# A new hand-written instruction order for the first of two spectral + MLP layers, with the negated third of a table made earlier

## The chip, the cores and the metric

The kernel runs on one core of a Trainium2 chip. The core has a matrix engine (TensorE, PE in the profile), a vector engine (VectorE, DVE), an activation engine (ScalarE, ACT), a general engine (GpSimd, POOL) and a queue engine for transfers (SyncE, SP). The metric is the device time of one execution in microseconds; lower is better.

## The reference, cut to what matters

Two blocks, A and B, are applied twice in turn to a state `x` of 2048 rows and 512 columns (bf16).

```python
def _A_ref(x, w_r, w_i):                       # spectral filter
    X = rfft2(x.astype(float32))               # over rows and columns
    X = X * (w_r + 1j * w_i)                   # 2048 x 257 weights
    return irfft2(X, s=(S, D)).astype(bfloat16)

def _B_ref(x, w1, w2, w3, w4):                 # mixer and MLP, F = 1792
    h = gelu(layernorm(x) @ w1)
    # four column groups of h are shifted by +1, -1, +2, -2 rows
    x1 = x + concat(shifted h) @ w2
    return x1 + gelu(layernorm(x1) @ w3) @ w4

x = x + _A_ref(layernorm(x), w_r, w_i);  x = x + _B_ref(layernorm(x), w1, w2, w3, w4)
x = x + _A_ref(layernorm(x), w_r, w_i);  x = x + _B_ref(layernorm(x), w1, w2, w3, w4)
```

## The kernel before, in words

The 2048 rows are held as 128 partitions by 16 columns-of-rows, called q. The Fourier transforms are matrix products with tables. One call of `layer` is one spectral block and one MLP block; it is called twice, with the order string `ORDER_A` for the first layer and `ORDER_B` for the second. Nothing schedules the kernel but these strings (the tile framework is in manual schedule mode): a token is one step, steps are recorded in the order of the string, and each engine carries out its own steps in that order. The number after a dot is the PSUM bank (of eight) that a step's products write. A trailing A or V says whether ACT or DVE does a copy or a normalization.

The tokens, by stage:

- **Forward spectrum, weights, first half of the way back.** `d` (line 462, PE) transforms the columns of unit u (a unit is one or two of 16 frequency blocks b); `t` (ACT or DVE) copies the result out as `TV`; `q` (line 486, PE) does the rest of the row transform with the table `TL`; `x` copies it out as `X`; `p` (`weigh`, line 501, DVE) multiplies `X` by the weights `W`, once with the real plane (pl 0) and once with the imaginary one (pl 1), into `PB`; `b` (`back_q`, line 510, PE) multiplies `PB` by the table `TR`, eight products to a block; `m` (`take_b`) copies block b into `M`.
- **The made third of the table.** `TR` has three parts. Two are loaded from DRAM (line 180, in two halves of 16 frequencies), and the third is minus the first: `N0` and `N1` (`negate`, line 698, DVE) make it for blocks 0 to 7 and 8 to 15. Every second product of a `b` reads it.
- **Second half of the way back, first norm.** `D` (line 528, PE) needs all of `M`; `Y` copies out; `P` (line 540, PE); `a` (line 548, DVE) adds to x; `s` (line 258, ACT) sums squares; `r` and `c` (POOL) make the norm's factors for four q; `n` normalizes; `T` (SP) turns two q by a transposing DMA.
- **MLP.** `v` (line 579) is the product with w1, `h` its gelu (ACT), `u` (line 595) the product with w2 over shifted rows, `f`, `k`, `E`, `R`, `o`, `U` the residual and the second norm, `w` (line 630) the product with w3, `g` (line 637, ACT) its gelu, `W` (line 643) the product with w4, `A` (line 648, DVE) the add to x. `L` (`permute`, DVE) rearranges a part of `W` for the second layer.
- **Seam to the second layer.** `B`, `j`, `S` (statistics on DVE, factors on POOL), `Q` (DVE, a scaled table), `O` (lines 349 to 361, PE, the next layer's first transform), `G` (copies into `V`), `X` (zero products that fill PE). The second layer's first `d` needs all of `V`.

The small buffers are few, and a step that reuses one waits for its last reader: `TV` and `Y` share three, `X` has two, `PB` has eight slots (two to a `p`).

How the weights arrive: `load_all` queues all loads on SP in one fixed order, each chunk of `W` covering four blocks (blocks 0 to 3, 4 to 7, 8 to 11, 12 to 15), real plane first. A chunk lands in partitions 0 to 63, and a second DMA, issued by POOL (line 209), copies it to partitions 64 to 127. `weigh` needs both. After the last of them a small gate DMA (line 187) lets the four MLP weights start. Neither the loads nor the POOL copies are in the order string.

Of the kernel before, what the change touches and what calls it, by code (L numbers as in the profile page):

```python
# [13 lines left out]
BF16 = dt.bfloat16  # L14
FP32 = dt.float32

P = 128
# [81 lines left out]
def kernel(  # L99
# [26 lines left out]
    load_all(K, A_x, A_w_r, A_w_i, B_w1, B_w2, B_w3, B_w4)  # L126
    make_hT(K)
    wake(K)
    first_front(K)
    for last in (False, True):  # L130
# [88 lines left out]
def wake(K):  # L219

    nc = K.nc
    t = K.const.tile([P, 256], BF16, name="zeros")
    nc.vector.memset(t[:], 0.0)
    one = K.small.tile([P, 1], FP32, name="wake")
    nc.scalar.activation(one[:], K.eps[:], ACT.Sqrt, bias=0.0, scale=1.0)
    K.zeros = t
    fill(K, WAKE)


def fill(K, n):  # L230
    for i in range(n):
        K.nc.tensor.matmul(K.ps[:, 7 if K.bank is None else K.bank, 0:256], lhsT=K.zeros[:, 0:P], rhs=K.zeros[:], start=True, stop=True)


class Stats:
# [155 lines left out]
def first_front(K):  # L391
# [26 lines left out]
    def front(k):  # L418
        ps[k] = over_p(K, FIRST[k])
        if k in FILL:  # L420
            fill(K, FILL[k])
# [19 lines left out]
def layer(K, last):  # L441
# [265 lines left out]
    for op in (ORDER_B if last else ORDER_A).split():  # L707
        op, _, bank = op.partition(".")
        K.bank = int(bank) if bank else None
        if op[0] == "X":  # L710
            fill(K, int(op[1:]))
            continue
        if op[0] in FLEX:
            table[op[0]](int(op[1:-1]), op[-1])
        else:
            table[op[0]](int(op[1:]))
# [16 lines left out]
Q15V O3 Q14V G4A O5 G3V O7 G5A O8 G8A G7V  # L733
"""
ORDER_A = """
d4.0 d1.2 d2.4 t1A q1.2 t2A t4V x1V q4.0 d10.6 q2.4 x4A p1 t10V d6.2 d12.0 q10.6 x2A t6A p4 N0 d8.4 q6.2 t12A t8A
b1.0 x10V d15.1 p2 b4.6 b3.7 m1A x6A b5.0 m4A t15V d14.1 q8.2 m3A b2.6 p10 d0.7 m5A N1 p6 q12.4 b10.0 t14V x8A
q15.2 x12A t0A p8 m2A x15A b11.1 m11A p12 q0.4 b6.7 b8.6 m6A p15 x0A q14.2 x14V b7.1 m10A b9.7 m7A m9A b13.4 p0
b15.5 b12.0 p14 m15A m15V m12A b0.1 b14.7 m8V m13V m0A m14A D2.4 D3.6 Y3A D0.0 Y2V P4.4 a4 Y0A P7.5 P6.6 P5.7 D1.0
a7 a6 a5 D4.4 s4 P0.6 Y1V s7 P1.7 s6 a0 s5 P3.0 Y4A r1 a1 P2.1 s0 a3 P8.6 P9.7 a2 D5.4 a8 D7.0 n7V n6V n5V T3 s1  # L740
n4V s3 s2 T2 r0 a9 D6.2 Y5A P11.6 Y7A s8 P10.4 P15.5 Y6A P13.7 a11 a10 s11 n2V n3V a15 n0V P14.6 n1A a13 c1 s10
P12.4 s9 r2 a12 s15 L7 a14 v3.2 n10V s12 n9V s13 s14 T1 v2.4 h3 n8A T0 n11V L12 r3 h2 n12V v1.6 h1 v0.2 T5 h0 c0
n15V n14A u3.6 T4 u2.7 u1.2 v5.4 f1 n13V u0.3 L15 h5 v4.0 f2 T7 T6 f3 E2 f0 u4.2 E3 v6.6 h4 k1 f4 L6 L1 v7.2 k3
u5.0 E4 c3 u6.1 k0 f5 E0 u7.4 k2 c2 R0 h7 h6 E1 o0V f6 k4 o1V o2A u10.5 u9.0 f7 u8.1 o3V u14.4 u12.6 f10 k5 f8
u11.1 U0 L9 k6 k7 f9 u13.5 R1 E5 u15.0 f12 E7 f14 f13 U1 E9 E8 w4.6 o4A E6 f11 L5 o5V o6V o7A w0.4 k10 k8 k9 w5.2
g0 E13 w1.4 f15 E14 k12 U3 E11 k11 k13 U2 g4 E12 k14 w2.0 E10 w6.6 R2 g5 w7.2 g1 o9V g7 o11V g6 k15 w3.4 g2 o10A R3
g3 o8A L0 w13.2 w9.6 w12.0 L3 w11.4 o14A E15 U4 g13 g12 L10 o13V U5 g11 W1.0 g9 W2.1 W3.6 L11 o15A w10.4 w8.2 L4
g10 o12V L2 L13 A1 g8 L8 A3 A2 W0.4 w14.2 A0 B2 W5.5 B0 L14 B3 g14 U6 W7.4 A5 B1 A7 B7 w20.2 w19.4 j1 j2 W6.0 j0 j7
g19 W4.1 U7 A6 g20 w15.2 w24.4 w21.6 B5 A4 g21 g15 w16.0 B6 j3 B4 w17.6 w23.2 g16 j6 w27.0 j5 g17 g27 w18.6 j4 g18
S0 w25.0 Q0 W9.6 Q3 S1 W10.7 g25 A10 g24 Q2 B10 w22.4 W8.7 Q1 g23 A9 Q4 O1.2 g22 Q7 w26.4 Q6 B9 W11.6 O0.0 G1A j9  # L750
Q5 g26 G1V A8 B8 O2.4 G0A A11 B11 G2A j11 W14.7 W12.6 j10 G2V A14 B14 j14 j8 G0V A12 S14 Q14 B12 W15.7 j12 A15 B15
j15 W13.6 O14.7 S2 S12 Q9 Q11 O3.0 Q12 S15 Q8 Q10 O4.4 G14A G3A Q15 A13 B13 G4A j13 G3V S13 O5.6 X4.2 O15.2 Q13 G4V
G15V G5A G15A X4.3 O6.6 G6A X8.3
"""
ORDER_B = """
d15.0 t15A d4.2 q15.0 x15V d1.4 t4A d8.6 t1A q1.4 q4.2 p15 t8A x1V b15.0 d12.6 x4A p1 m15V m15A q8.4 t12A d10.0
# [45 lines left out]
```

## Time and profile before

| | us |
|---|---|
| median of 13 runs | 368.7 |
| lowest and highest of them | 366.07 and 369.82 |
| the profiled execution | 368.84 |
| its span in the profile | 366.9 |
| PE busy in the span | 344.6 (94%) |
| DVE busy | 183.7 (50%) |
| ACT busy | 198.9 (54%) |
| POOL busy | 67.0 (18%) |
| granted TensorE clock, mean | 0.986 |

All times in this text are microseconds from the start of the span of that one execution. Busy is the time in which an engine has an instruction in work[...]. In a timeline row, the first number is the start, the second the length, `x8` the number of instructions merged, and the bracket how long the engine had been idle and who ended that.

The first layer's frequency stage runs from 22.91 (first `d`) to 52.99 (first `D`), its middle up to 98.24 (first `w`), its MLP up to about 196.4 (last `W`), and the second layer's first `d` starts at 202.71.

### The profile page before, as it was taken

The page shows a single profiled execution, that of the slowest core. Times are in us where ns is not written, and L with a number is a line of the kernel's source. Part 1 is how long each engine was busy: PE and PEld are TensorE (multiplying, and loading weights), DVE is VectorE, ACT ScalarE, POOL GpSimd, SP SyncE. Part 2 cuts the span into 40 slices and gives each one's busy share as a digit, 9 for nine tenths or more (in the row PEclk, how much of TensorE's full clock was granted, in tenths as well). Part 3 has the DMA queues.
Part 4 walks back from the last instruction along what each step waited for, and adds up shares of the span by engine and source line. Part 5 has one row for each costly group of instructions (what it writes and reads, how often), then busy time and mean ns, then how long its engine had stood idle before and what let it go on. Part 6 is the DMA issues. An engine that isn't in the chain of part 4 may idle for free.

```text
span 366.9 us, 5596 instructions
## 1 busy us (share of the span) xinstructions
PE 344.6 (94%) x2107; PEld 189.8 (52%) x2124; DVE 183.7 (50%) x453; ACT 198.9 (54%) x343; POOL 67.0 (18%) x171
## 2 busy tenths in 40 slices
PE   7798599889999999999999999999999999999996
PEld 5576378534444444444446678734444444444442
DVE  4856568838985243400688697855690021100022
ACT  5867469978679230154213897996786420247100
POOL 1211003782341000200022000782440000000000
PEclk9899889999999999999999999999999999999999
DMA  7999493641332500000000000363313032000012
GB/s 232 232 202 214 105 372 123 114 87 30 58 58 38 107 0 2 0 0 2 1 0 2 2 2 0 61 115 59 57 30 58 0 57 73 0 29 2 29 43 86
DMA packets 47274, 24.60 MB, mean 67 GB/s; under 512 B 34832, under 2 KB 44048, under 8 KB 47248
## 3 DMA queue, kind: packets, MB, share of 16 engines
q1 hardware_dynamic: 46464, 22.09, 26.5%
q0 software_dynamic: 640, 2.10, 2.7%
q8 instruction: 16, 0.26, 0.3%
q14 instruction: 10, 0.08, 0.1%
q10 hardware_dynamic: 144, 0.07, 0.1%
HBM read 11.67 MB, written 2.10 MB: 38 GB/s over the span
## 4 chain that ended last, share of the span: by engine, by line
PE 73%; DMA 11%; ACT 9%; DVE 3%; issue 2%; SPq 1%; POOL 0%; ACTq 0%; DVEq 0%; POOLq 0%
PE ps L630 26%; PE ps L643 25%; PE ps L595 8%; PE ps L579 5%; ACT junk L258 4%; DMA W<-in_A_w_i_dram 3%; PE ps L510 3%; DMA W<-W 2%; DMA TL<-tab_TL 2%; PE ps L462 2%; DMA W<-in_A_w_r_dram 2%; PE ps L486 2%; PE ps L528 2%; ACT Y L149 1%; SPq L166 1%
## 5 line engine op out<-in xcount | busy, mean ns | idle before, releaser
L637 ACT ACTIVATE gT<-ps 128x1024 bf16<-128x1024 f32 x56 | 54.9, 1023 | 86.5 <-PE ps L630 86.5
L630 PE MATMUL ps<-xT,w 128*128 128x512 bf16 x448 | 98.7, 379 | 0.0
L643 PE MATMUL ps<-w,gT 128*128 128x512 bf16 x435 | 97.8, 379 | 0.7
L648 DVE TENSOR_TENSOR x_state<-ps,x_state 128x512 bf16<-128x512 f32 x32 | 21.7, 689 | 121.1 <-PE ps L643 121.0
L630 PEld LDWEIGHTS <-w 128*128 128x128 bf16 x448 | 43.8, 98 | 52.6
L643 PEld LDWEIGHTS <-gT 128*128 128x128 bf16 x448 | 43.8, 98 | 52.6
L579 PE MATMUL ps<-xT,w 128*128 128x512 bf16 x128 | 29.1, 379 | 1.5 <-ACT hT L586 0.9
L603 DVE SCALAR_TENSOR_TENSOR xn<-xn,ln_c,ps 128x512 bf16<-128x512 bf16 x32 | 23.1, 743 | 13.3 <-PE ps L595 9.0
L595 PE MATMUL ps<-w,hT 128*128 128x512 bf16 x124 | 28.8, 379 | 1.0 <-ACT hT L586 0.8
L501 DVE TENSOR_TENSOR PB<-X,W 128x1024 bf16<-128x1024 bf16 (+1 forms) x40 | 21.3, 579 | 7.8 <-DMA W<-W 4.2
L510 PE MATMUL ps<-TR,PB 128*128 128x128 bf16 x256 | 19.1, 232 | 5.6 <-DVE TR L698 4.6
L258 ACT ACTIVATE junk<-x_state 128x512 bf16<-128x512 bf16 x36 | 22.6, 629 | 1.1
L548 DVE SCALAR_TENSOR_TENSOR x_state<-ps,x_state 128x512 bf16<-128x512 f32 x32 | 20.4, 686 | 3.5 <-PE ps L540 3.5
L258 ACT ACTIVATE junk<-xn 128x512 bf16<-128x512 bf16 x32 | 20.1, 627 | 3.6 <-DVE xn L603 3.1
L586 ACT ACTIVATE hT<-ps 128x512 bf16<-128x512 f32 x32 | 17.5, 607 | 7.9 <-PE ps L579 7.9
L246 DVE BATCH_NORM_STATS2 ln_st<-x_state 128x6 f32<-128x512 bf16 x28 | 18.8, 685 | 4.8 <-DMA x_state<-in_A_x_dram 4.6
L510 PEld LDWEIGHTS <-PB 128*128 128x128 bf16 x256 | 16.3, 104 | 9.3 <-issue 4.8
L579 PEld LDWEIGHTS <-w 128*128 128x128 bf16 x128 | 12.4, 98 | 16.7 <-issue 1.5
L595 PEld LDWEIGHTS <-hT 128*128 128x128 bf16 x128 | 12.4, 98 | 16.4 <-ACT hT L586 1.1
L149 ACT ACTIVATE V<-ps 128x1024 bf16<-128x1024 f32 (+2 forms) x11 | 9.5, 885 | 15.8 <-PE ps L351 14.2
L281 POOL TENSOR_SCALAR ln_ve<-ln_mv 128x4 f32<-128x4 f32 (+1 forms) x15 | 3.9, 261 | 76.9 <-DVE ln_mv L274 76.2
L462 PE MATMUL ps<-FA,V 128*128 128x256 bf16 x128 | 16.3, 273 | 1.7 <-ACT V L149 1.7
(73 smaller groups left out, 389.0 us busy)
## 6 DMA issues: line engine op xcount, KB each, us to landing
w<-in_B_w_dram SPq DMA_DIRECT2D x2, 1792.0 KB, 12.3
x_state<-in_A_x_dram SPq DMA_DIRECT2D x8, 256.0 KB, 5.8
W<-W POOLq DMA_DIRECT2D x8, 256.0 KB, 8.8
out_dram<-x_state SPq DMA_DIRECT2D x16, 128.0 KB, 1.8
TR<-tab_TR SPq DMA_DIRECT2D x2, 512.0 KB, 10.0
w<-in_B_w_dram SPq DMA_DIRECT2D x2, 512.0 KB, 4.5
W<-in_A_w_r_dram SPq DMA_DIRECT2D x7, 128.0 KB, 11.0
W<-in_A_w_i_dram SPq DMA_DIRECT2D x7, 128.0 KB, 10.5
```

The source lines that it names most:

```text
L258: K.nc.scalar.activation(junk[:], src, ACT.Square, bias=0.0, scale=D ** -0.5, accum_out=self.s[:, i, 1:2])
L462: nc.tensor.matmul(oi[:, 1 - h], rhs=K.FA[:, t, h], lhsT=V[:, 2 * t + h, 2 * b:2 * b + 2].rearrange("d b q c -> d (b q c)"), start=(t == 0 ...
L501: nc.vector.tensor_tensor(t[:, :, 0:n], x, w, op=ALU.mult)
L510: nc.tensor.matmul(o[:, (2 * h + F) * P:(2 * h + F + 1) * P], lhsT=pab[u][k][:, h, b - u, F * P:(F + 1) * P], rhs=K.TR[:, k:k + 2, 2 * b + ...
L548: nc.vector.scalar_tensor_tensor(K.x[:, q, :], ps.pop(("P", q)), 1.0, K.x[:, q, :], op0=ALU.mult, op1=ALU.add, accum_out=ln[g].s[:, i, 0:1])
L579: nc.tensor.matmul(o[:, i], lhsT=K.w1[:, t, j * P:(j + 1) * P], rhs=xT[g][:, :, t, :], start=(t == 0), stop=(t == 3))
L595: nc.tensor.matmul(o, lhsT=K.hT[:, j, st:st + P], rhs=K.w2[:, j, :], start=(j == 0), stop=(j == 3))
L603: nc.vector.scalar_tensor_tensor(xn[:, q, :], xn[:, q, :], ln[q // 4].c[:, q % 4:q % 4 + 1], ps.pop(("u", n)), op0=ALU.mult, op1=ALU.add, ...
L630: nc.tensor.matmul(o[:, i], lhsT=K.w3[:, c, t * P:(t + 1) * P], rhs=xT3[g][:, :, c, :], start=(c == 0), stop=(c == 3))
L637: nc.scalar.activation(gT[g][:, 2 * j:2 * j + 2, :], ps.pop(("w", k)), ACT.Gelu_apprx_tanh, bias=0.0, scale=1.0)
L643: nc.tensor.matmul(o, lhsT=gT[g][:, t, i * P:(i + 1) * P], rhs=K.w4[:, t, :], start=(t == 0), stop=(t == 13))
L648: nc.vector.tensor_tensor(K.x[:, q, :], ps.pop(("W", n)), K.x[:, q, :], op=ALU.add)
```

## The change

`ORDER_A` is replaced by another order of the same steps, with other banks and here and there another engine for a copy. `ORDER_0` (everything before the first layer) and `ORDER_B` are untouched. In the frequency stage the first units are now 1, 0, 4, 6, 2; `N0` stands before `p4` instead of after it, and `N1` before `p10` instead of after it. The `p` steps come as 0, 1, 4, 6, 2, 10, 8, 12, 14, 15 (before: 1, 4, 2, 10, 6, 8, 12, 15, 0, 14). At the seam, row q = 0 (`W14`) is now the last product of the MLP instead of row 15 (`W13`), so `O14`, one row, comes last instead of `O6`, two rows. Apart from that the zero tile of the filling products is 128 columns instead of 256, read twice.

```diff
 def wake(K):
-    t = K.const.tile([P, 256], BF16, name="zeros")
+    t = K.const.tile([P, P], BF16, name="zeros")
 def fill(K, n):
     for i in range(n):
-        K.nc.tensor.matmul(K.ps[:, 7 if K.bank is None else K.bank, 0:256], lhsT=K.zeros[:, 0:P], rhs=K.zeros[:], start=True, stop=True)
+        K.nc.tensor.matmul(K.ps[:, 7 if K.bank is None else K.bank, 0:256], lhsT=K.zeros[:], rhs=K.zeros[:].unsqueeze(1).to_broadcast([P, 2, P]), start=True, stop=True)
 ORDER_A = """
-d4.0 d1.2 d2.4 t1A q1.2 t2A t4V x1V q4.0 d10.6 q2.4 x4A p1 t10V d6.2 d12.0 q10.6 x2A t6A p4 N0 d8.4 q6.2 t12A t8A
-b1.0 x10V d15.1 p2 b4.6 b3.7 m1A x6A b5.0 m4A t15V d14.1 q8.2 m3A b2.6 p10 d0.7 m5A N1 p6 q12.4 b10.0 t14V x8A
-q15.2 x12A t0A p8 m2A x15A b11.1 m11A p12 q0.4 b6.7 b8.6 m6A p15 x0A q14.2 x14V b7.1 m10A b9.7 m7A m9A b13.4 p0
-b15.5 b12.0 p14 m15A m15V m12A b0.1 b14.7 m8V m13V m0A m14A D2.4 D3.6 Y3A D0.0 Y2V P4.4 a4 Y0A P7.5 P6.6 P5.7 D1.0
-a7 a6 a5 D4.4 s4 P0.6 Y1V s7 P1.7 s6 a0 s5 P3.0 Y4A r1 a1 P2.1 s0 a3 P8.6 P9.7 a2 D5.4 a8 D7.0 n7V n6V n5V T3 s1
-n4V s3 s2 T2 r0 a9 D6.2 Y5A P11.6 Y7A s8 P10.4 P15.5 Y6A P13.7 a11 a10 s11 n2V n3V a15 n0V P14.6 n1A a13 c1 s10
-P12.4 s9 r2 a12 s15 L7 a14 v3.2 n10V s12 n9V s13 s14 T1 v2.4 h3 n8A T0 n11V L12 r3 h2 n12V v1.6 h1 v0.2 T5 h0 c0
-n15V n14A u3.6 T4 u2.7 u1.2 v5.4 f1 n13V u0.3 L15 h5 v4.0 f2 T7 T6 f3 E2 f0 u4.2 E3 v6.6 h4 k1 f4 L6 L1 v7.2 k3
-u5.0 E4 c3 u6.1 k0 f5 E0 u7.4 k2 c2 R0 h7 h6 E1 o0V f6 k4 o1V o2A u10.5 u9.0 f7 u8.1 o3V u14.4 u12.6 f10 k5 f8
-u11.1 U0 L9 k6 k7 f9 u13.5 R1 E5 u15.0 f12 E7 f14 f13 U1 E9 E8 w4.6 o4A E6 f11 L5 o5V o6V o7A w0.4 k10 k8 k9 w5.2
-g0 E13 w1.4 f15 E14 k12 U3 E11 k11 k13 U2 g4 E12 k14 w2.0 E10 w6.6 R2 g5 w7.2 g1 o9V g7 o11V g6 k15 w3.4 g2 o10A R3
-g3 o8A L0 w13.2 w9.6 w12.0 L3 w11.4 o14A E15 U4 g13 g12 L10 o13V U5 g11 W1.0 g9 W2.1 W3.6 L11 o15A w10.4 w8.2 L4
-g10 o12V L2 L13 A1 g8 L8 A3 A2 W0.4 w14.2 A0 B2 W5.5 B0 L14 B3 g14 U6 W7.4 A5 B1 A7 B7 w20.2 w19.4 j1 j2 W6.0 j0 j7
-g19 W4.1 U7 A6 g20 w15.2 w24.4 w21.6 B5 A4 g21 g15 w16.0 B6 j3 B4 w17.6 w23.2 g16 j6 w27.0 j5 g17 g27 w18.6 j4 g18
-S0 w25.0 Q0 W9.6 Q3 S1 W10.7 g25 A10 g24 Q2 B10 w22.4 W8.7 Q1 g23 A9 Q4 O1.2 g22 Q7 w26.4 Q6 B9 W11.6 O0.0 G1A j9
-Q5 g26 G1V A8 B8 O2.4 G0A A11 B11 G2A j11 W14.7 W12.6 j10 G2V A14 B14 j14 j8 G0V A12 S14 Q14 B12 W15.7 j12 A15 B15
-j15 W13.6 O14.7 S2 S12 Q9 Q11 O3.0 Q12 S15 Q8 Q10 O4.4 G14A G3A Q15 A13 B13 G4A j13 G3V S13 O5.6 X4.2 O15.2 Q13 G4V
-G15V G5A G15A X4.3 O6.6 G6A X8.3
+d1.0 d0.1 d4.2 t1A t0V q0.0 x0V q1.4 d6.6 x1V t4A p0 d2.0 t6A q4.4 d10.2 t2V q6.6 x4A p1 N0 p4 d8.4 t10A t8V x6A p6
+q2.0 b1.2 b4.3 m1A d12.6 b0.2 m4A d14.3 x2A q10.4 t12A p2 d15.0 b5.1 t14V x10A m0V q8.6 b2.3 b6.4 x8A m2A m6A m5A
+q12.6 q14.2 N1 p10 b7.5 t15A p8 b10.4 m7V b11.1 b3.0 x12A m11A x14V p12 p14 m3A b8.5 m8A q15.6 m10A b9.2 x15A p15
+b12.3 b13.5 m12A m9A b14.4 m13V b15.3 m15V m14A m15A D0.2 D1.4 Y1A Y0V D3.6 P1.2 P0.3 P2.4 a1 P3.5 Y3A a0 a2 a3
+D2.6 D4.2 Y2V P6.4 s1 P7.5 a6 a7 s0 P4.6 s2 P5.7 D7.0 s3 a5 a4 D5.4 r0 Y4A n2V s6 P8.7 s7 s5 P9.6 n3V s4 D6.2 Y7A
+n1V a8 Y5A n0V Y6A P10.7 r1 P11.4 a9 P13.5 a10 P15.6 T1 n5V T0 n4V n6A P12.7 n7V s10 a11 T2 T3 a12 s9 a15 P14.2 s11
+s8 a13 s13 s15 v0.0 c1 v1.4 a14 v3.2 s14 s12 r2 r3 c0 h1 n10V h0 v2.4 n11V h3 n9V T5 h2 n8V u0.2 n13V L3 n12A u1.3
+u2.4 n14A n15A T4 f0 v5.0 h5 T6 v4.6 E0 u3.2 f1 L5 f2 c2 u4.3 h4 L7 f3 k1 T7 E3 k2 u5.6 f4 k0 k3 R0 f5 v7.4 v6.6
+L13 E2 h7 u15.4 u7.5 k4 E1 f15 h6 o3V E4 u6.6 o0V E15 o1V k15 f6 u12.4 u11.7 f7 c3 f11 U0 o2A u8.6 k6 f8 u13.5 E5
+f13 k5 E11 u9.7 E8 k7 k8 u10.6 u14.5 k11 R1 U1 f9 E6 f12 f10 w6.2 o6A f14 E12 E7 E9 k10 L2 o5V w0.6 w3.4 L8 k9 E10
+o7V g0 R2 w5.6 k12 w4.0 E13 o4A k13 U2 g3 g4 w1.4 o9A E14 g1 o11V L15 w2.0 L6 L1 g5 k14 g2 R3 U3 w7.4 g6 w9.6 g7 L9
+w8.2 w10.4 g9 L12 o15A o8V W0.6 o12A g8 W3.7 o10V w12.2 A0 w13.0 L11 o13A W1.6 g13 g12 g10 A3 U4 o14V A1 w11.2 g11
+U5 w14.6 B3 W5.2 W7.3 W2.4 B0 A5 W4.2 L4 B5 A7 j3 j0 L14 B7 B1 W6.3 U7 A2 w15.4 A4 j1 g14 w17.6 g15 B2 A6 j5 j2
+w16.4 g16 U6 B6 B4 S0 Q1 w20.2 w18.4 g18 L0 g17 j7 w19.0 g20 w21.4 j4 j6 S1 Q7 Q2 g19 Q3 w24.2 Q4 w22.0 g21 O1.4
+G1A W9.6 g24 w26.2 g22 Q0 Q5 Q6 A9 G1V B9 w25.6 j9 w23.4 g26 g25 W10.6 W11.7 A10 g23 O3.4 G3A A11 B11 O2.2 L10 j11
+w27.0 B10 G3V W8.6 A8 B8 g27 j8 j10 W15.7 A15 W13.6 S2 O0.4 Q9 W12.7 G2A Q10 B15 G2V Q11 A13 G0A Q8 G0V W14.6 j15
+B13 O4.4 j13 A12 O5.2 S15 B12 Q15 S13 j12 O15.7 S12 Q13 Q12 G4A A14 B14 j14 G15V S14 Q14 G5A X4.0 O6.0 X4.6 O14.6
+G6A G4V G15A G14A X8.2
```

## The prediction

> **What bounds the kernel now.** I read the engine table first (PE 344.6 of 366.9), then the chain of waits that ended last, then the timelines of PE and DVE where PE was not full. PE is full from 80 to 196 and in the second layer's MLP. The order of the first layer can matter in three places: the frequency stage (22.91 to 52.99), the middle (to 98.24), and the seam (last `W` to 202.71).
>
> The chain through the frequency stage, in order of time (start, length, what):
>
> ```profile
> 19.43 12.36 DMA W<-in_A_w_i_dram
> ...
> 32.34 8.84 DMA W<-W
> ...
> 41.20 0.69 DVE PB L501
> 41.89 0.35 DVE TR L698
> ...
> 42.28 0.82 PE ps L510 x7
> ```
>
> The imaginary weights of blocks 8 to 11 are complete at 41.20. Behind them wait one multiplication (`p10`, second half), then `N1`, and only then PE. DVE and PE, from their timelines:
>
> ```profile
> 30.08 0.69 DVE L501 TENSOR_TENSOR PB<-X,W 128x1024 bf16<-128x1024 bf16 x1 [1.15 <-ACT TV L149]
> 31.58 0.69 DVE L501 TENSOR_TENSOR PB<-X,W 128x1024 bf16<-128x1024 bf16 x1 [0.81 <-DMA W<-W]
> ...
> 37.56 0.69 DVE L501 TENSOR_TENSOR PB<-X,W 128x1024 bf16<-128x1024 bf16 x1 [1.96 <-issue]
> 41.20 0.69 DVE L501 TENSOR_TENSOR PB<-X,W 128x1024 bf16<-128x1024 bf16 x1 [2.95 <-DMA W<-W]
> ```
> ```profile
> 32.66 0.55 PE L510 MATMUL ps<-TR,PB 128*128 128x128 bf16 x7 [1.00 <-DVE TR L698]
> ...
> 38.46 0.23 PE L510 MATMUL ps<-TR,PB 128*128 128x128 bf16 x1
> 42.28 0.82 PE L510 MATMUL ps<-TR,PB 128*128 128x128 bf16 x7 [3.60 <-DVE TR L698]
> ...
> 52.99 2.78 PE L528 MATMUL ps<-G,M 128*128 128x256 bf16 x24 [0.88 <-DVE M L147]
> ```
>
> All four DVE rows are `p4` and `p10` waiting for weights. The releasers of the first and third do not fit: the POOL copies of those planes were issued at 21.14 and 28.63, and 8.9 later (the imaginary one took 8.84) is 30.04 and 37.53. While DVE stood at `p10`, `p6` stood behind it, whose weights had been there since 31.58. PE was idle for 3.60, and paid again:
>
> ```profile
> 40.00:42.00 2.00, 0.00 (x0) 0.06 (x1) 0.80 (x2) 0.01 (x1) 0.00 (x0) 1.00 0.54 115
> 42.00:44.00 2.00, 1.39 (x11) 0.86 (x12) 2.00 (x5) 1.17 (x2) 0.00 (x0) 0.60 0.01 2
> 44.00:46.00 2.00, 1.46 (x12) 0.97 (x11) 2.00 (x5) 2.00 (x4) 0.00 (x0) 0.50 0.46 127
> 46.00:48.00 2.00, 2.00 (x20) 1.71 (x20) 1.20 (x3) 1.76 (x4) 0.00 (x0) 0.50 1.05 343
> 48.00:50.00 2.00, 2.00 (x26) 1.59 (x27) 1.43 (x4) 1.28 (x4) 0.00 (x0) 0.69 1.03 383
> ```
>
> (Busy of PE, PE weight load, DVE, ACT, POOL; then the granted clock.) It is about half from 42.5 to 49.2. Sixteen `b` products took 1.89 there and about 1.05 at full clock.
>
> **The change part by part.** Loads and POOL copies keep their order, so weights land as before: 30.05 and 31.58 (blocks 4 to 7), 37.5 and 41.20 (8 to 11), by about 42.9 (12 to 15: the gate behind them issued at 42.97). I walked the new order on all engines, each step at the latest of its engine, its input and its buffer's last reader, with row durations: a two-block `d` 0.95, `q` 0.54, `b` 0.53; ACT `t` 1.3, `x` 0.93, `m` 0.5; DVE `t` 1.3, `x` 1.2, `m` 0.65, two-block `p` half 0.62, `N` 0.35.
>
> *Blocks 0 to 7.* `p0` ends at 27.65 (its imaginary plane lands at 27.28, as in the old rows), `t2V` 28.9, `p1` 29.5, `N0` 29.85. `N0` now lies in the wait of `p4` for 30.05 and costs nothing; without that cover it is 0.35. `p4` still ends at 32.2, where `b4` waits 0.85 instead of 1.0 for `N0`. Then `t8V` 33.45, `p6` 34.7, `p2` 35.95, `t14V` 36.6, `m0V` 37.25, `N1` 37.6. `N1` needs the second half of `TR`: issued at 20.62, at most 13.1 to landing, so 33.7. It costs nothing ahead of `p10`, which waits for 37.53. On PE this feeds b1, b4, b0, b5, b2, b6, b7 and d12, d14, d15, q10, q8, q12, q14, up to 39.5. Then `b10` stands: 39.6 to 41.9, a gap of 2.3 instead of 3.6. Queued behind DVE's wait are `p8`, `m7V`, `x14V`, `p12`; all need later weights or are short.
>
> *After 41.20.* Old: PE had eleven `b` and three `q` left, DVE thirteen multiplications (six of half size), a `t`, an `x`, `N1`. New: nine `b` and one `q`; nine multiplications (four of half size): `p10` to 41.85, `p8` 43.1, `m7V` 43.7, `x14V` 44.35, `p12` 45.6, `p14` 46.25, `p15` 46.9. PE follows: b8 44.3, q15 44.6, b9 45.15, b12 46.2, b13 46.7, b14 47.25, b15 47.8. Last `m` 48.4. First `D` at **48.5** instead of 52.99: 4.5 less, some 3 of it the half clock.
>
> [...] The trace shows gaps up to 1.0 with the clock at 1.00 after, and 3.60 with half after; 2.3 lies between. [...] nine `b` costing 1.05 each: about 2.5 more, 51.0. In this trace 32 to 34 had PE busy 1.19 of 2.0 and the clock stayed 1.00, so I take 48.5 and keep 51.0.
>
> [...] `N1` and `p6` move to where POOL issues the copies at 32.34 and 36.42[...]. The row: the POOL copies took 509 to 775 ns, 512 in the middle, the one at 32.34 beside `N0` 0.51. I take nothing.
>
> *Middle, D to the first w: 45.25 before.* It is bound by ACT: six `Y`, sixteen `s`, one `n`, then the gelu table (1.28) at 72.80, 19.8 after the first `D`, without a gap from 54.94. The new order has the same six, sixteen and one there, and its first `Y` is also ready after two `D`, at 1.95. Then three `h` (1.0 each) open the first `u`: 24.1 (before: 24.4, with a normalization of 0.7 among the three). From there 16 `u` and 4 `v` at 0.216 a product are 20.7. **45.0**, -0.25. The transposes T1, T0 come at 59.0 by this clock; the MLP weights, gated at 43 as before, finish by 58.2 (DMA share 1.05 at 57, 0.27 at 58), so they just miss each other; overlap would cost at most v0's slack, about 0.6, before it counts. `N`, `L` and residuals moved on DVE lie in its idle time (50% busy).
>
> *MLP, 98.2 before.* 448 products at 0.216 are 96.7, and four `O` of 8 short products (0.45) stand before the last `W` instead of three: 98.5, +0.3 to +0.45. `g` takes 1.0 for each 1.73 of `w`; I found no `w` or `W` whose bank or gelu comes late.
>
> *Seam, 6.27 before (196.44 to 202.71).*
>
> ```profile
> 202.71 1.48 PE L462 MATMUL ps<-FA,V 128*128 128x256 bf16 x12 [1.01 <-ACT V L149]
> ```
>
> Before, PE work of 5.26 and this idle 1.01, waiting for the last copies into `V`. Now after `W14`: O4 0.45, O5 0.87, O15 0.43, fills, O6 0.87, fills, O14 0.43, fills: 4.78. The chain A14, B14, j14, G15V, S14, Q14 (0.69 + 0.69 + 0.18 + 0.41 + 0.9 + 0.28, less overlap) lets O14 go at 3.5; `G14A`, half a unit, ends at 4.95. **5.0**, -1.27, of which 0.45 went ahead of the last `W`.
>
> Zero tile: same product shape, DVE's set of 0.17 lies before any input: 0, bounded by ±0.1.
>
> Sum: -4.5 - 0.25 + 0.4 - 1.3 = -5.7. The profiled execution (368.84, 1.94 outside its span) becomes 363.1; the median, 0.14 lower, **363.0**. The second layer keeps its order and length.
>
> **The rivals.**
> *Half clock or a slipped landing remains (0.17).* The stretch after 41.9 at half clock[...]: 363.0 + 2.5 = 365.5; with 0.5 lost in the middle 366. For: low PE use from 32 to 42. Against: the clock held there.
> *The order does less than it says (0.08).* The weights at 41.20 stay the bound, and what follows is as long as before, only `N0` and `N1` leaving the path: 0.15 + 0.35 and the seam's 0.8: 367.4 to 368.5. Against: two `b` and four multiplications fewer are left at 41.9, and PE's gap is shorter.
> *Slower (0.10): the half clock spreads into D and P.* If PE at 42 to 48, now sparser, does not win its clock back before 48.5, the 128 products of 0.109 there take 27.9 instead of 13.95. PE has about 5 of slack under ACT, so 9 come through: 363 + 2.5 + 9 = 374.5. It decides if more than about two thirds of D and P run at half. Against: before, 6.7 at half clock were enough.
> *More (0.05).* The middle or the seam gains another 1 to 2: under 361.
>
> **How the numbers follow.** Likeliest (0.60): 363.0, own range 361.5 to 364.5. The range 360.8 to 367.4 leaves out the slower rival, most of "does less", and 0.03 below. 0.3% (1.1 us, about what a measurement here can tell from no change) puts the borders at 367.6 and 369.8. Faster: 0.60 + 0.17 + 0.05 + 0.02 = 0.84; same 0.06; slower 0.10.
>
> **What would show it.** Right: `N` no longer a releaser of PE at line 510; one PE gap near 40 of 2 to 2.6, ended by a DVE `PB`; granted clock 1.00 from 42 to 50; first `D` near 48.5, first `w` near 93.5, seam near 5. Wrong: weights of blocks 8 to 11 later than 41.5, a clock of 0.5 after 42, or a first `w` later than 96.

## The result, and the profile after

The new kernel takes 363.38 us (median of 11 runs, 361.24 to 364.34). The kernel before, with the runs that came later, takes 367.98 (median of 48). The ratio is 0.9867, 95% interval 0.984 to 0.9893: faster, by 4.9 with 3.9 to 5.9 between the ends (the two medians alone are 4.6 apart). A second build of the same kernel on another chip gave 0.9904 (0.9867 to 0.9941), 3.5. The forecast was 363.0, range 360.8 to 367.4.

The profiled execution took 362.16, its span is 360.1 (before: 366.9), its mean granted clock 0.995 (before: 0.986). One profile used further down, that of the new order with the third made late, comes from a slow execution, 3.6 above the median of its kernel, in which the weights landed late; of it single rows are read, not its length.

| from the start of the span | before | after | difference of the stretch |
|---|---|---|---|
| first `d` | 22.91 | 22.62 | -0.29 |
| imaginary weights of blocks 8 to 11 complete | 41.20 | 38.42 | -2.49 |
| first `D` | 52.99 | 45.85 | 11.79 to 7.43: -4.36 |
| first `w` | 98.24 | 91.37 | 45.25 to 45.52: +0.27 |
| second layer's first `d` | 202.71 | 194.96 | 104.47 to 103.59: -0.88 |
| end | 366.9 | 360.1 | 164.2 to 165.1: +0.9 |

The sum is -6.8. The second row was not made by the change: no load was moved. In the ten other profiles that wait for these weights they were complete between 36.67 and 41.32, on average at 38.8 with the old order in this stage and at 38.7 with the new one. So of the profile's 6.8 about 2.5 is this execution's earlier landing, and the rest, 4.3, lies between the 3.5 and the 4.9 of the two comparisons.

VectorE, where the prediction showed the two waits and `N1` behind the second (start, length, what; in the bracket the idle time before and its releaser):

```profile
29.01 0.42 DVE L698 TENSOR_SCALAR TR<-TR 128x1024 bf16<-128x1024 bf16 x1
29.34 0.69 DVE L501 TENSOR_TENSOR PB<-X,W 128x1024 bf16<-128x1024 bf16 x1
30.21 0.69 DVE L501 TENSOR_TENSOR PB<-X,W 128x1024 bf16<-128x1024 bf16 x1 [0.18 <-DMA W<-W]
...
35.75 0.42 DVE L698 TENSOR_SCALAR TR<-TR 128x1024 bf16<-128x1024 bf16 x1
36.08 0.69 DVE L501 TENSOR_TENSOR PB<-X,W 128x1024 bf16<-128x1024 bf16 x1
38.42 1.90 DVE L501 TENSOR_TENSOR PB<-X,W 128x1024 bf16<-128x1024 bf16 x3 [1.66 <-issue]
```

`N0` and `N1` (L698) now stand ahead of the multiplications that wait. The row at 38.42 is the second half of `p10`, and `p8`'s two halves follow at once. TensorE:

```profile
37.50 0.68 PE L510 MATMUL ps<-TR,PB 128*128 128x128 bf16 x9
39.17 1.46 PE L510 MATMUL ps<-TR,PB 128*128 128x128 bf16 x23 [1.00 <-DVE PB L501]
40.97 0.61 PE L510 MATMUL ps<-TR,PB 128*128 128x128 bf16 x8 [0.34 <-DVE M L147]
...
42.77 2.07 PE L510 MATMUL ps<-TR,PB 128*128 128x128 bf16 x31 [0.26 <-DVE PB L501]
45.85 2.36 PE L528 MATMUL ps<-G,M 128*128 128x256 bf16 x20 [1.00 <-ACT M L149]
```

The gap of 3.60 that `N1` ended has become one of 1.00 that the weights themselves end. Only nine blocks' products stand behind it. The stretches of 2 us (length; busy of PE, PE weight load, DVE, ACT, POOL; granted clock; DMA share and rate) show no half clock:

```profile
38.00:40.00 2.00, 1.00 (x19) 0.83 (x17) 1.58 (x3) 1.52 (x3) 0.00 (x0) 1.00 0.35 88
40.00:42.00 2.00, 1.66 (x27) 1.22 (x25) 2.00 (x4) 1.69 (x4) 0.00 (x0) 1.00 0.01 4
42.00:44.00 2.00, 1.74 (x31) 1.57 (x30) 1.93 (x6) 1.87 (x5) 0.00 (x0) 1.00 0.45 111
44.00:46.00 2.00, 1.00 (x15) 0.65 (x13) 1.25 (x3) 1.34 (x3) 0.00 (x0) 1.00 1.06 352
```

The chain through the stage still runs over the imaginary weights and their POOL copy. Behind `p10` it has turned: before it went on with `N1` and PE, now with copies.

```profile
30.07 6.10 DMA W<-W
...
36.78 1.64 issue
38.42 0.70 DVE PB L501
...
42.83 0.60 ACT X L149
43.43 1.53 ACT M L149 x3
```

One row of it should be read with care: the 1.64 before 38.42 is put down to "issue". In the second profile of the new kernel the same row waits too, and there it is the copy of `W`, so 38.42 is read as the landing (the copy that POOL issued at 30.07 took 8.3 to land, which is 38.4):

```profile
39.11 1.90 DVE L501 TENSOR_TENSOR PB<-X,W 128x1024 bf16<-128x1024 bf16 x3 [0.79 <-DMA W<-W]
```

The stage is still bound by the landing, and after it by copies more than by products.

The seam, last `W` to the second layer's first `d`, has lost its idle 1.01 (189.85 is the first `O` behind the last `W`; the next 12 rows of `O` have 0.27 each and start 0.11 apart, so what one product costs is read from the starts):

```profile
189.85 0.61 PE L361 MATMUL ps<-Tq,x_state 128*128 128x128 bf16 x8
...
194.96 1.48 PE L462 MATMUL ps<-FA,V 128*128 128x256 bf16 x12
```

### The profile page after: what moved, and what is told of

Same layout as the page of the kernel before. It is cut to its first block, busy times and chain, and to the rows that moved or that the text cites. A ratio compares the mean times of both kernels' runs of the same rounds, so it can differ in the third digit from the quotient of the medians.

```text
span 360.1 us, 5599 instructions
## 1 busy us (share of the span) xinstructions
PE 341.6 (95%) x2106; PEld 188.1 (52%) x2124; DVE 183.0 (51%) x453; ACT 200.4 (56%) x343; POOL 66.3 (18%) x171
## 3 DMA queue, kind: packets, MB, share of 16 engines
q1 hardware_dynamic: 46464, 22.09, 27.3%
## 4 chain that ended last, share of the span: by engine, by line
PE 74%; ACT 10%; DMA 9%; issue 3%; DVE 2%; SPq 1%; ACTq 0%; DVEq 0%; POOLq 0%
PE ps L630 27%; PE ps L643 27%; PE ps L595 7%; PE ps L579 5%; ACT junk L258 4%; DMA W<-in_A_w_i_dram 3%; DMA TL<-tab_TL 2%; PE ps L462 2%; DMA W<-W 2%; ACT Y L149 2%; PE ps L528 2%; ACT M L149 1%; DMA W<-in_A_w_r_dram 1%; PE ps L510 1%; PE ps L486 1%
## 5 line engine op out<-in xcount | busy, mean ns | idle before, releaser
L595 PE MATMUL ps<-w,hT 128*128 128x512 bf16 x124 | 28.6, 379 | 0.5 <-ACT hT L586 0.2
L595 PEld LDWEIGHTS <-hT 128*128 128x128 bf16 x128 | 12.5, 98 | 15.8 <-ACT hT L586 0.9
L510 PE MATMUL ps<-TR,PB 128*128 128x128 bf16 x256 | 17.1, 219 | 1.6 <-DVE PB L501 1.3
L540 PE MATMUL ps<-Y,Tinv 128*128 128x256 bf16 x128 | 15.5, 272 | 1.6 <-ACT Y L149 1.6
L528 PE MATMUL ps<-G,M 128*128 128x256 bf16 x128 | 15.3, 273 | 1.9 <-ACT M L149 1.9
```

Source lines behind the costliest of these rows:

```text
L510: nc.tensor.matmul(o[:, (2 * h + F) * P:(2 * h + F + 1) * P], lhsT=pab[u][k][:, h, b - u, F * P:(F + 1) * P], rhs=K.TR[:, k:k + 2, 2 * b + ...
L528: nc.tensor.matmul(o[:, i, e * 256:(e + 1) * 256], lhsT=M[:, F, e, 2 * m + i, :], rhs=K.G[:, F, e, :], start=(F == 0), stop=(F == 1))
L595: nc.tensor.matmul(o, lhsT=K.hT[:, j, st:st + P], rhs=K.w2[:, j, :], start=(j == 0), stop=(j == 3))
```

## The experiments

Each kernel ran in five rounds against the kernel before on the same chip. The chips differ a little (the kernel before: 365.98, 365.78 and 366.28 on the three that were used), so the ratio counts. The theory: the gain is the frequency stage's, because less is queued behind the late weights and because TensorE keeps its clock. The rivals: the early third alone makes it; the middle and the seam do; it is only weights that happened to land early; the new order is shorter whether or not weights are late.

"After landing" is from the second half of `p10` to the first `D`. The last column counts the executions whose mean granted clock was 0.994 or more. In the new kernel's profile, at 0.995, the only half clock ahead of the last work is one of 3.41 from 11.40, before the stage. A lower mean can also come from a longer one there, as in the profile of the new order without weight waits (0.989, half clock for 6.8 from 10.5). In the first comparison the new kernel's clock was full in 8 of 12.

| kernel | median | ratio, 95% | landing | after landing | clock full |
|---|---|---|---|---|---|
| before, three chips | 365.98, 365.78, 366.28 | 1 | 41.20 | 11.79 | 4 of 44, 3 of 31, 2 of 27 |
| new order in the frequency stage alone | 362.98 | 0.9913 (0.9882 to 0.9944) | 39.27 | 7.42 | 8 of 11 |
| all but the frequency stage | 365.71 | 1.001 (0.999 to 1.003) | 38.53 | 11.92 | 2 of 22 |
| third early alone | 365.66 | 0.9991 (0.9964 to 1.0018) | 37.88 | 11.11 | 1 of 14 |
| new kernel again | 363.42 | 0.9904 (0.9867 to 0.9941) | 39.11 | 7.42 | 8 of 10 |
| old with zero products in the gap | 365.26 | 0.9979 (0.9957 to 1.0001) | 36.71 | 10.26 | 14 of 22 |
| new with the third late | 362.09 | 0.9907 (0.9872 to 0.9941) | 41.32 | 8.26 | 9 of 10 |
| old, no weight waits | 360.34 | 0.9849 (0.9799 to 0.9899) | none | none | 4 of 6 |
| new, no weight waits | 361.01 | 0.9885 (0.9839 to 0.9932) | none | none | 2 of 6 |
| old, weights meant to be later | 366.03 | 0.9987 (0.9966 to 1.0008) | 39.77 | 12.82 | 2 of 22 |
| new, weights meant to be later | 361.41 | 0.9866 (0.9831 to 0.99) | 37.21 | 7.42 | 6 of 6 |
| new, `m7` on ACT | 361.68 | 0.9881 (0.9843 to 0.9919) | 36.67 | 7.05 | 6 of 6 |

**New order in the frequency stage alone.** The new tokens up to the last `m`, the old ones from there on, the old zero tile.

```diff
-d4.0 d1.2 d2.4 t1A q1.2 t2A t4V x1V q4.0 d10.6 q2.4 x4A p1 t10V d6.2 d12.0 q10.6 x2A t6A p4 N0 d8.4 q6.2 t12A t8A
+d1.0 d0.1 d4.2 t1A t0V q0.0 x0V q1.4 d6.6 x1V t4A p0 d2.0 t6A q4.4 d10.2 t2V q6.6 x4A p1 N0 p4 d8.4 t10A t8V x6A p6
...
 D2.4 D3.6 Y3A D0.0 Y2V P4.4 a4 Y0A P7.5 P6.6 P5.7 D1.0
```

> The new order up to the last copy into M, the old order from the first D on. If the gain lies in the frequency stage (4.5 by the prediction: a shorter gap of PE, so no half clock, and less work left behind the last weights): about 4.2 less than before, first D between 46 and 48.5, clock 1.00 from 38 to 50. If the early weights of the one profiled run of the new kernel (blocks 8 to 11 complete by 38.4 instead of 41.2) made most of it: about 2 less, and the first D late again wherever the weights land near 41.

Measured 0.9913: about 3.2 of the 3.5 that the whole change gave on that chip, and not told apart from it. TensorE:

```profile
40.02 1.46 PE L510 MATMUL ps<-TR,PB 128*128 128x128 bf16 x23 [1.64 <-DVE PB L501]
...
46.69 1.49 PE L528 MATMUL ps<-G,M 128*128 128x256 bf16 x12 [1.00 <-ACT M L149]
```

The landing is 1.9 earlier than in the trace of before, but the first `D` 6.3 earlier, and 7.42 after the landing as in the new kernel. The old seam is back with its idle 1.01, and the middle takes the old 45.26. So the frequency stage carries nearly all of the gain. The clock stayed at 1.00 through the gap of 1.64 (length; busy of PE, PE weight load, DVE, ACT, POOL; clock; DMA):

```profile
38.08:41.50 3.42, 1.75 (x29) 1.47 (x27) 2.23 (x4) 2.30 (x4) 0.00 (x0) 1.00 0.40 86
```

**All but the frequency stage.** The other half of the same cut: old tokens up to the last `m`, new ones behind. The zero tile is the old one here too, so neither half holds the new one; its products take the same 0.60 for four and 1.04 for eight in the profiles of before and after.

```diff
 b15.5 b12.0 p14 m15A m15V m12A b0.1 b14.7 m8V m13V m0A m14A
-D2.4 D3.6 Y3A D0.0 Y2V P4.4 a4 Y0A P7.5 P6.6 P5.7 D1.0
+D0.2 D1.4 Y1A Y0V D3.6 P1.2 P0.3 P2.4 a1 P3.5 Y3A a0 a2 a3
```

> The old order up to the last copy into M, the new one from the first D on. By the prediction: middle 0.25 less, MLP 0.4 more, seam 1.3 less, about 1.1 less than before in all; the gap of PE of about 3.6 and the half clock are back. If the later stages carry the gain: 3 or more less.

Measured 1.001: nothing. Its weights landed at 38.53, as early as the new kernel's, and yet:

```profile
39.61 0.57 PE L510 MATMUL ps<-TR,PB 128*128 128x128 bf16 x7 [3.40 <-DVE TR L698]
...
50.45 1.80 PE L528 MATMUL ps<-G,M 128*128 128x256 bf16 x15 [0.88 <-DVE M L147]
```
```profile
36.60:40.02 3.42, 0.41 (x7) 0.47 (x7) 1.49 (x3) 0.70 (x1) 0.00 (x0) 1.00 0.41 98
40.02:46.84 6.82, 5.73 (x50) 4.12 (x48) 5.45 (x11) 4.98 (x9) 0.00 (x0) 0.50 0.74 238
```

Gap, releaser, half clock and the 11.9 after the landing are those of before. That takes the early landing away as the cause. The seam did get shorter here (MLP with seam 103.59 against 104.47); the middle took 0.25 more and the second layer 0.4 more, so that about 0.2 of the 1.1 expected was left, under what was measurable.

**The third early, alone.** The old order, `N0` ahead of `p4` and `N1` ahead of `p10`.

```diff
-p4 N0 d8.4
+N0 p4 d8.4
...
-b2.6 p10 d0.7 m5A N1 p6
+b2.6 N1 p10 d0.7 m5A p6
```

> The old order, with N0 moved ahead of p4 and N1 ahead of p10 and nothing else. By the prediction's steps N0 gives up to 0.35 and N1 0.35 on the path: about 0.5 less than before, if the gap of PE (3.6 less about 0.4) still brings the half clock; if the shorter gap of about 3.2 keeps the clock at 1.00, about 3 less. If the made third is the whole change: 4 to 5 less.

Measured 0.9991: nothing that shows in the time; the profile has 0.7 less after the landing. Its rows tell most about the clock:

```profile
38.63 0.56 PE L510 MATMUL ps<-TR,PB 128*128 128x128 bf16 x7 [0.70 <-DVE PB L501]
39.74 0.40 PE L486 MATMUL ps<-TV,TL 64*128 64x256 bf16 x4 [0.55 <-ACT X L149]
40.47 0.61 PE L510 MATMUL ps<-TR,PB 128*128 128x128 bf16 x8 [0.33 <-DVE TV L147]
41.90 0.61 PE L486 MATMUL ps<-TV,TL 64*128 64x256 bf16 x4 [0.82 <-ACT TV L149]
42.44 1.89 PE L510 MATMUL ps<-TR,PB 128*128 128x128 bf16 x16
```
```profile
38.02:41.44 3.42, 1.57 (x19) 1.21 (x20) 3.42 (x6) 2.27 (x3) 0.00 (x0) 1.00 0.22 47
41.44:44.85 3.41, 2.95 (x25) 1.94 (x25) 2.11 (x5) 3.17 (x7) 0.00 (x0) 0.50 0.90 291
```

`N1` no longer releases PE, the gap of 3.60 is gone, and no gap from 37 to 42 is over 0.82. But DVE is full, feeding PE one copy and one multiplication at a time, and PE, busy 1.57 of the 3.42 us up to 41.44, loses its clock there all the same. Making the third early removes the wait and not its consequence.

**The new kernel again.** No edit; it shows how far one profile repeats.

> The new kernel once more. 4.6 less than before (ratio 0.987). If its early weights were chance, this profile shows blocks 8 to 11 complete somewhere between 38 and 42; if the change brings them forward, again near 38.4.

Landing 39.11, 7.42 later the first `D`, clock full, middle 45.52, MLP with seam 103.58: three stretches repeat to 0.01.

**The old order with zero products in the gap.** Twenty zero products (2.2 at full clock) ahead of `b10` keep PE busy where it stood.

```diff
-N1 p6 q12.4 b10.0 t14V x8A
+N1 p6 q12.4 X20.0 b10.0 t14V x8A
```

> The old order with 20 filling products (2.2 of PE work) ahead of b10, where PE stands for 3.4 to 3.6 waiting for weights. Nothing else moves. If the idle gap brings the half clock and the half clock costs about 3: the clock stays at 1.00 from 38 to 50, the first D comes 8.5 to 9 after the weights of blocks 8 to 11 instead of 11.8, and the whole is 2.5 to 3 less. If sparse use brings it also without a long gap (as in the run with only the made third moved, where no gap was over 1.0 and the clock was half for about 3): some of the half clock stays and about 1.5 is gained. If the clock is no part of it: no change.

```profile
36.65 2.36 PE L232 MATMUL ps<-zeros 128*128 128x256 bf16 x20
38.84 0.61 PE L510 MATMUL ps<-TR,PB 128*128 128x128 bf16 x8
...
46.97 1.25 PE L528 MATMUL ps<-G,M 128*128 128x256 bf16 x10 [0.95 <-DVE M L147]
```

The clock stayed at 1.00 from 36 to 48, and in 14 of 22 executions it was full, where on this chip it was in 3 of 31 before. But the time moved by 0.5 to 0.8 only, not by the gain expected. Part of the reason stands in the rows: this time the weights were complete at 36.71 and `N1` ended at 37.7, so that the zero products, started at 36.65, held `b10` for 1.1. After the landing 10.26 went by; if the held 1.1 was passed on in full, 9.1 without it, against 11.8 to 11.9 with the half clock. So the half clock's price in the old order is about 2.7, and what remains from 9.1 to the new order's 7.4, some 1.7, is the shorter queue behind the weights. Both are estimates that rest on this one profile and on that "if". A filler of fixed length isn't a way to collect the 2.7, as it sits in the path whenever the weights come early.

**The new order with the third late.** `N0` and `N1` put back behind `p4` and `p10`.

```diff
-x4A p1 N0 p4 d8.4
+x4A p1 p4 N0 d8.4
...
-q12.6 q14.2 N1 p10 b7.5
+q12.6 q14.2 p10 N1 b7.5
```

> The new order with N0 behind p4 and N1 behind p10 again. By the prediction's steps N0 was worth 0.35 of DVE before t8V, and N1 0.35 on the chain behind the last weights: first D 7.7 after the weights instead of 7.4, clock still 1.00, 0.3 to 0.7 more than the new kernel (ratio to before about 0.990). If making the third early carries the change: 3 or more of the gain is gone.

```profile
32.42 1.00 PE L510 MATMUL ps<-TR,PB 128*128 128x128 bf16 x15 [1.50 <-DVE TR L698]
...
40.59 0.23 PE L510 MATMUL ps<-TR,PB 128*128 128x128 bf16 x1 [0.75 <-DVE PB L501]
42.41 2.82 PE L510 MATMUL ps<-TR,PB 128*128 128x128 bf16 x31 [1.59 <-DVE TR L698]
```

The two waits for L698 are back on PE, as they should be. The time is not: 0.9907, the same as the new kernel's 0.9904. With the third early alone at 0.9991, both sides say that the early third is worth less than these runs can measure.

A clock of 1.00 was expected, and the profiled execution does not have it. The weights landed at 41.32, PE stood for 0.75 and 1.59 with little between, and the clock was half from 43.32 to 46.73:

```profile
39.90:43.32 3.42, 1.14 (x18) 1.10 (x19) 2.63 (x5) 1.60 (x2) 0.00 (x0) 1.00 0.15 34
43.32:46.73 3.41, 3.41 (x32) 2.65 (x30) 3.31 (x7) 2.67 (x5) 0.00 (x0) 0.50 0.47 142
```

The first `D` came 8.26 after the landing, where 7.7 was expected. This is the one profile in which the new order, but for `N0` and `N1`, met weights as late as in the trace of before. In the nine other executions the clock was full.

**No weight waits.** `weigh` always reads the first real plane, which is there early, so the output is another. Both orders.

```diff
-w = K.W[:, pl, 2 * u:2 * u + 2 * n].rearrange
+w = K.W[:, 0, 0:2 * n].rearrange
```

> The old order, with every weigh step reading the first plane of blocks 0 to 3, which has landed before the first of them; so the weights never make anything wait, and the output is another. If the old order's loss is the wait for late weights and the half clock behind it: no PE gap over 1.5, clock 1.00, first D near 43, and 5 to 7 less than before.

> The new order, weights read as in the run with the old order without weight waits. If the new order's gain is that it has less left behind late weights, it has no lead in the frequency stage here: first D within 1 of the old order's, and only the seam's 0.9 less. If the new order is better in itself, the lead of about 4 in the first D stays.

From the first `d` to the first `D` the old order takes 21.44 (22.09 to 43.53), the new one 21.89 (24.19 to 46.08), both at full clock. Without late weights the new order has no lead in these two profiles, it is 0.45 behind, and the two times are not told apart. Its gain is only in how it stands to the weights. The old kernel then paid elsewhere, in a place that the prediction had called a near miss. Its transposes started at 54.18, while the MLP weights were still being loaded (the DMA moved 349 GB/s from 54 to 56); one took 6.3 to land, where they took 3.1 to 3.3 in the trace of before. PE stood for it, and its clock was half from 62.41 to 65.82:

```profile
61.57 4.65 PE L579 MATMUL ps<-xT,w 128*128 128x512 bf16 x13 [2.42 <-DMA xT<-xn]
```
```profile
58.99:62.41 3.42, 1.00 (x6) 0.48 (x5) 2.64 (x8) 3.29 (x10) 2.10 (x6) 1.00 1.00 204
62.41:65.82 3.41, 3.41 (x9) 1.21 (x8) 2.09 (x5) 3.35 (x8) 2.60 (x8) 0.50 0.65 122
```

Its middle took 47.35, 2.1 more than before. Being early by more than the loads allow is partly taken back.

**Weights meant to land later.** The second halves of `TR` and the table `G` queued ahead of the chunks of blocks 8 to 11, in both orders.

```diff
     for lo in range(0, NH, 8):
+        if lo == 16:
+            table("G", nc.sync)
+            nc.sync.dma_start(K.TR[:, 0:2, 16:32], dram["TR"][:, :, 16:32])
```

> The old order, with the loads of G and of the second half of TR queued ahead of the weights of blocks 8 to 11 instead of behind them: those weights land some 3 later, the total loaded is the same. First D 11.8 after they land, half clock as before, the whole about 3 more than before.

> The new order with the same later weights. PE's gap ahead of b10 becomes 4 to 5. [...] clock 0.5 for 3 to 7 after it, first D about 10 after the weights instead of 7.4, so some 5 to 6 more than the new kernel. If the new order's short chain behind the weights does not feel the clock (DVE leads it): 7.4 to 8.4, some 3 more than the new kernel.

This missed. What the edit put off was the real plane, whose copy POOL issued at 33.40 and 32.65 (elsewhere between 24.75 and 30.92). The imaginary weights came at 39.77 and 37.21, inside the range seen without the edit, so the pair says nothing on how each order bears later weights. It does repeat the other numbers: 7.42 after the landing and full clock in the new order, 12.82 and half clock in the old.

**`m7` on ACT.** In the new order DVE copies `m7` between the multiplications of `p8` and `p12`; here ACT does it, right behind `b7`.

```diff
-b7.5 t15A p8 b10.4 m7V b11.1
+b7.5 m7A t15A p8 b10.4 b11.1
```

> The new order, with the copy of block 7 into M made by ACT in its wait instead of by DVE between p8 and x14V, where it lies on the chain behind the last weights. DVE's chain is 0.6 shorter: first D 6.8 after the weights instead of 7.4, and the whole 0.4 to 0.7 less than the new kernel, which the times can hardly tell; no change in the first D if another engine leads by then.

```profile
36.67 1.90 DVE L501 TENSOR_TENSOR PB<-X,W 128x1024 bf16<-128x1024 bf16 x3 [2.11 <-issue]
39.31 2.79 DVE L501 TENSOR_TENSOR PB<-X,W 128x1024 bf16<-128x1024 bf16 x6
```

`p12` starts 2.64 after the landing instead of 3.02, and the first `D` 7.05 after it instead of 7.42. In time 0.9881 (0.9843 to 0.9919) isn't told apart from the new kernel. It shows which engine holds the rest of the stage: DVE, by what stands between its multiplications. A version better by a measurable amount was not found.

## Why the prediction was right, step by step

*What is left behind the late weights.* Forecast 7.3 from the landing to the first `D`; measured 7.43, then 7.42 in three further profiles. This step carried the forecast, and the frequency stage alone (0.9913) and the rest alone (1.001) show that it is where the gain lies.

*"Some 3 of it the half clock".* About 2.7 in the stage, by the kernel with zero products less what they held. The kernel before gives a second, weaker sign: its nine executions at full clock have medians of 364.35, 364.23 and 364.13 on the three chips, 1.6 to 2.2 under those of the others there (365.98, 365.94, 366.28); earlier weights in these nine can be a part of that. The other part, 1.7, is then what the products, multiplications and copies moved ahead of the wait are worth.

*Where the forecast got help.* "39.6 to 41.9, a gap of 2.3" came out as 1.00, and the prediction's sign, a gap "of 2 to 2.6", failed. The walk behind it was right: PE's work ahead of `b10` ends 8 after the second half of `p4` starts (31.58 to 39.5 forecast, 30.21 to 38.17 measured). What it took as fixed, the distance between the weights of blocks 4 to 7 and those of 8 to 11, is not: 9.62 before, 8.21 here, 8.90 in the new kernel's second profile, 8.68 in the frequency stage alone, 8.54 with `m7` on ACT. The gap is 1.00, 1.25, 1.64 and 1.51, which is 7.0 to 7.7 less than the distance; at the 9.62 of before it would be 2 to 2.6, an estimate from these four. So the weights of the profiled executions came early enough to spare the step that chose 48.5 over 51.0 its test, and that was luck. The nearest to a test is the new order with the third late, at a distance of 9.98. There the step failed: the clock fell. It did not cost the 2.5 of the prediction's other case either: from the landing to the first `D` it was 8.26 instead of 7.42, and `N1` behind `p10` is a part of this 0.84.

*The clock.* The prediction chose between two cases, 48.5 with the clock held and 51.0 with nine `b` at half clock. That a gap of 2.3 would keep the clock was its author's estimate between a gap of 1.0 and one of 3.60, with PE busy for 1.19 of 2.0 at full clock beside it. The traces give more. Before, the changes of the clock from 11.68 on lie 3.41, 27.31, 6.83 and 317.44 apart, after, 3.41 and 344.75: whole multiples of 3.41. The half clocks shown above of four experiments last 3.41 (third early, third late, old without weight waits) or 6.82 (all but the frequency stage). No long gap is needed for a half clock: with the third early the clock fell at 41.44 behind gaps of at most 0.82.

Laid over the traces in steps of 3.41 from these changes, the stretches show what went with it, how long PE was busy in one:

| stretch at full clock | PE busy | clock in the next |
|---|---|---|
| before, 38.99 to 42.40 | 0.12 | 0.50 |
| all but the frequency stage, 36.60 to 40.02 | 0.41 | 0.50 |
| old, no weight waits, 58.99 to 62.41 | 1.00 | 0.50 |
| third late, 39.90 to 43.32 | 1.14 | 0.50 |
| third early alone, 38.02 to 41.44 | 1.57 | 0.50 |
| frequency stage alone, 38.08 to 41.50 | 1.75 | 1.00 |
| after, 233.27 to 236.68 | 1.93 | 1.00 |
| after, 38.71 to 42.12 | 2.60 | 1.00 |

In the traces of before and after no other stretch from 15 on has less than 1.93, but for the last one ahead of each end (0.26 and 0.48, half clock behind both). In the new kernel's profile PE was busy for 2.71 and 2.60 in the two from 35.30 to 42.12, and the gap of 1.64 in the frequency stage alone left it 1.75. The prediction's number came out with PE that busy; its own gap of 2.3 did not occur. By this count such a gap would leave PE at most 1.1 of a stretch if it fell into one, and more if it lay across two (an estimate, 3.41 less 2.3).

*POOL's copies beside DVE.* The prediction took nothing for a landing, and nothing was seen: the four copies that POOL issued at 26.22, 30.07, 33.34 and 36.23 took it 0.51 each, the one at 36.23 beside `p10`. None of them ran beside `N0` (29.01 to 29.43) or `N1` (35.75 to 36.17), so for `N1` this was no test.

*The made third.* Forecast at no cost ahead of the waits, and 0.35 each behind them. The runs agree that it is small; without either move the time stays the same.

*Middle.* Forecast -0.25, measured +0.27, and the same 45.50 to 45.53 in every profile with the new order there. The first `u` (L595) starts 24.39 after the first `D`, as late as before, where 24.1 was forecast. The term that failed is the gelu table's 19.8 after the first `D`, taken over from the old order:

```profile
63.34 0.63 ACT L258 ACTIVATE junk<-x_state 128x512 bf16<-128x512 bf16 x1 [0.36 <-DVE x_state L548]
66.34 1.28 ACT L586 ACT_TABLE_LOAD   x1
```
```profile
61.50 5.51 PE L579 MATMUL ps<-xT,w 128*128 128x512 bf16 x24 [0.18 <-DMA xT<-xn]
68.28 1.89 PE L579 MATMUL ps<-xT,w 128*128 128x512 bf16 x8 [1.28 <-ACT hT L586]
70.24 1.24 PE L595 MATMUL ps<-w,hT 128*128 128x512 bf16 x4
71.72 1.69 PE L595 MATMUL ps<-w,hT 128*128 128x512 bf16 x7 [0.23 <-ACT hT L586]
```

ACT comes to the table at 66.34, 20.49 after the first `D`, and on the way waits 0.36 for an addition of DVE. From the table's end to the first `u` it is 2.6 where three `h` of 1.0 were forecast, which gives back a part. From the first `u` to the first `w` it is 21.1 where 20.7 was forecast, 0.23 of it the last row's wait. Transposes and MLP weights did nearly "just miss each other": the wait for `xT` is 0.18.

*MLP and seam.* Forecast +0.4 and 5.0 for the seam. With the end of the last `W` as the border, as in the prediction (196.44 before, 190.01 after), it is 98.64 (+0.44) and 4.95 (-1.32). The stretch is 0.88 shorter against 0.9 forecast.

*"The second layer keeps its order and length".* Wrong by 0.4 to 0.9. The second `v` of layer two waits longer for its transposed input:

```profile
235.59 3.63 PE L579 MATMUL ps<-xT,w 128*128 128x512 bf16 x16 [1.48 <-DMA xT<-xn]
```

It was 0.56 before. In the five profiles in which the first layer's tokens are the old ones, but for `N0`, `N1` or zero products, this wait is 0.50 to 0.56 and the second layer takes 164.2. In the eight with any larger part of the new string, even the frequency stage alone or the rest alone, it is 1.02 to 1.48 and 164.6 to 165.1. The wait follows the landing of the fourth transpose (issued at 231.88 here, landed 3.66 later). It is late in two ways. In the six profiles read for it, 5.73 to 5.74 go by from the first transpose to the fourth in the three with old tokens behind the frequency stage (before, third early, frequency stage alone), 6.15 to 6.28 in the three with new ones (after, the new kernel again, all but the frequency stage). And it takes 3.39 to 3.66 to land in the three with the new frequency stage, 3.08 to 3.15 in the other three. In the trace of after one packet of instructions moves while it is under way, in that of before none (queue 14; packets, MB, share of the DMA engines):

```profile
q14 instruction: 1, 0.01, 0.9%
```

That this packet delays the transpose, or that the new strings bring it there, was not shown; no experiment was made on it.

*The rivals.* "Does less" did not come. The late half clock did not come in the new kernel's two profiles, nor did it spread into `D` and `P`: from 42 to 52 the granted clock was 1.00. With the third late it came, for 3.41, and ended before the first `D`.

## What to carry to other kernels

Where a transfer lands late, count what each engine has still queued behind it: work moved ahead of the wait pays once by itself, and here, by the estimate above, about one and a half times as much again by keeping TensorE busy enough for its clock. For the clock, add up how long PE is busy and do not look for the longest gap alone: here 1.57 of 3.42 with no gap over 0.82 lost it, and 1.75 with a gap of 1.64 kept it. One execution doesn't settle it: the new order with the third late lost the clock in its profile (mean 0.991) and had it full in the nine other executions (0.994 to 1.00). Taking the visible releaser off the wait (the made third) was worth nothing alone, since DVE, one copy and one multiplication at a time, still starved PE. Read a stage from the landing on and not from the start of the span: in four profiles with the new order there the landing moved by 2.1, while the time after it repeated to 0.01.

## What the runs showed of the hardware beyond that

- In the traces of before and after the granted clock changed at whole multiples of 3.41 from its other changes; a stretch at half clock lasted 3.41 (41.44 to 44.85 with the third early) or 6.83 (42.40 to 49.23 before).
- Whether the clock held went with how long PE was busy in such a stretch: 1.57 with no gap over 0.82 lost the clock (third early alone), 1.75 with a gap of 1.64 kept it (frequency stage alone). At half clock it came back after a stretch with PE busy for 2.95 (third early, 41.44 to 44.85) and 3.41 (before, 45.82 to 49.23), and not after one with 2.55 (before, 42.40 to 45.82). The busy times include modelled ends of products, so these numbers are those of this profile's count.
- The same queue of loads had its imaginary weights of blocks 8 to 11 complete between 36.67 (`m7` on ACT) and 41.32 (third late) from one profiled execution to the next.
- Transposing transfers issued from 54.18 on, while the MLP weights were loaded (old order without weight waits), took up to 6.3 to land, 3.1 to 3.3 in the trace of before. The fourth transpose of layer two took 3.39 to 3.66 in three profiles with the new frequency stage (after, its second profile, the frequency stage alone), 3.08 to 3.15 in three with the old one (before, third early alone, all but the frequency stage).
